# Attention and SwiGLU on one core: when each half of a batch is attended, and in which order its loads and steps are issued

## Chip, cores, metric

The kernel runs on one core of a Trainium2 chip. The metric is the device time of one execution in microseconds. The engines are TensorE (PE in the rows, PEld for its weight loads), VectorE (DVE), ScalarE (ACT), GpSimd (POOL) and SyncE (SP). GpSimd also issues almost all loads.

## The reference

Four batches, eight heads, 768 positions, head size 64. Each query sees the 8 first keys (global) and the 96 keys up to itself (local), with a slope per head times the distance as a bias; the rest is masked. The eight heads' results side by side are the 512 features of 3072 tokens, which go through a gated feed-forward layer.

```python
def _attn_ref(q, k, v, n_global, n_local) -> np.ndarray:
    ...
    scores = scale * np.matmul(q, k.transpose(0, 1, 3, 2))
    ...
    is_global = pos[None, :] < int(n_global)
    is_local = (rel >= 0) & (rel < int(n_local))
    keep = is_global | is_local
    ...
    scores = scores + bias[None, :, :, :]
    scores = np.where(keep, scores, -1000000000.0)
    scores = scores - np.max(scores, axis=-1, keepdims=True)
    a = np.exp(scores)
    a = a / (np.sum(a, axis=-1, keepdims=True) + 1e-09)
    return np.matmul(a, v).astype(np.float32)

def _moe_ref(x, w_gate, w_val, w_out) -> np.ndarray:
    g = x @ w_gate
    silu = g * (1.0 / (1.0 + np.exp(-g)))
    val = x @ w_val
    return (silu * val @ w_out).astype(np.float32)
```

## The kernel before

**Attention, in steps.** Heads go in pairs (`Pair`, four a batch). A pair's work is cut into steps, each a method: `transposes` turns q and k of two heads on TensorE, and copies bring them to `qT` and `kT` (L190, L196; L200 repeats the eight global key columns in each chunk). `scores(bk)` does a bank `bk` of three: the keys lie in seven chunks of 120 (plus the 8 global ones), each against at most 216 queries; two chunks fill bank 0, two bank 1, three bank 2. ScalarE takes the exponential (L220), and an engine `mul_eng` multiplies by a mask that holds the exponential of the bias or zero (L227, L231). `values(half, fast)` multiplies the result `at` by ones (`den`) and by V (`num`) for the queries of one half; VectorE turns `den` round, inverts it and spreads it (L259 to L262); the product goes to `xT`, on VectorE if `fast` (L267), else over a ScalarE copy to GpSimd (L270, L271). `HALF` says where a batch is cut. The first half reads banks 0 and 1, the second banks 1 and 2, so bank 1 is read by both.

**Feed-forward.** Tokens go in eight blocks of 384 (`TB`), two a batch. A block `t` is 12 times (for `f`) a gate group and a value group of four matmuls (`gate_or_val`), and from block 1 on a part of the output of block t - 1, three matmuls (`out_part`). I call each of these a group. ScalarE's tanh (L292) and VectorE (L294, L298) follow each gate and value group. Block `t` needs `xT` of its 384 tokens, all four pairs.

**What sets the order.** Engines take instructions in the order in which the program writes them. First `early` does the first half of batch 0 for the four pairs, staggered. Then the loop over `groups` writes the feed-forward groups, and puts attention steps from the list `todo` between them: each group adds its work times `quota` to `owed`, and each whole unit of `owed` takes one step. `due` holds how many steps must be through by the end of which block:

```python
due = {1: 8 + 24, 3: 24, 5: 24}
```

So the second half of batch 0 and all of batch 1 stand in blocks 0 and 1, batch 2 in blocks 2 and 3, batch 3 in 4 and 5; blocks 6 and 7 have no steps. Within a pair the steps are written one after the other (transposes, scores 0, 1, 2, values 0, 1), and a pair ends before the next begins.

**Loads.** `load_qk`, `load_v`, `load_w` and `load_wo` go through one queue of GpSimd; `loads` issues later ones at a given count 12 t + f. A `dma_start` waits until the one eight before it has landed, since eight semaphores go round (the order with its waits shows it). `load_globals` brings the eight global V rows into `vG`, and SyncE copies them into each `vS` from there.

## Time and profile before

| what | value |
|---|---|
| time, median of 3 runs | 294.28 us (293.05 to 294.45) |
| profiled execution | 293.91 us, its span 292.1 us |
| TensorE busy | 260.4 us (89%) |
| VectorE busy | 171.2 us (59%) |
| ScalarE busy | 142.8 us (49%) |
| GpSimd busy | 137.1 us (47%) |
| mean granted TensorE clock | 0.994 |
| chain that ended last | PE 64%, POOL 12%, DVE 11%, ACT 6%, DMA 4%, issue 3% |

The busy share is a mean over stages with different limits: before the first feed-forward group, in blocks with steps, in blocks without. The chain that ended last is followed back from the last instruction; it says which engine had the work that the rest waited for.

### The profile page before, as it was taken

The page shows a single profiled execution, that of the slowest core. Times are in us where ns is not written, and L with a number is a line of the kernel's source. Part 1 is how long each engine was busy: PE and PEld are TensorE (multiplying, and loading weights), DVE is VectorE, ACT ScalarE, POOL GpSimd, SP SyncE. Part 2 cuts the span into 40 slices and gives each one's busy share as a digit, 9 for nine tenths or more (in the row PEclk, how much of TensorE's full clock was granted, in tenths as well). Part 3 has the DMA queues.
Part 4 walks back from the last instruction along what each step waited for, and adds up shares of the span by engine and source line. Part 5 has one row for each costly group of instructions (what it writes and reads, how often), then busy time and mean ns, then how long its engine had stood idle before and what let it go on. Part 6 is the DMA issues. An engine that isn't in the chain of part 4 may idle for free.

```text
span 292.1 us, 5638 instructions
## 1 busy us (share of the span) xinstructions
PE 260.4 (89%) x2192; PEld 140.9 (48%) x2192; DVE 171.2 (59%) x349; ACT 142.8 (49%) x297; POOL 137.1 (47%) x162
## 2 busy tenths in 40 slices
PE   2538699799789999999989899999999999999983
PEld 1325345454445445545544545454555555555531
DVE  1627779986838565655663747474747655565510
ACT  4417644366366665556546374646475333322311
POOL 8845434057589637382988655555554100000000
PEclk9999999999899999999999999999999999999999
DMA  8999999907989110100799410101010100101111
GB/s 114 178 160 191 203 205 176 139 0 106 148 53 65 31 39 0 38 37 4 127 166 82 57 38 1 39 36 39 0 38 36 38 23 13 38 36 37 38 72 72
DMA packets 45402, 21.27 MB, mean 73 GB/s; under 512 B 28128, under 2 KB 42304, under 8 KB 45376
## 3 DMA queue, kind: packets, MB, share of 16 engines
q0 software_dynamic: 41376, 14.20, 44.9%
q1 hardware_dynamic: 4000, 6.72, 6.6%
q8 instruction: 17, 0.28, 0.4%
q14 instruction: 9, 0.07, 0.1%
HBM read 28.58 MB, written 6.29 MB: 119 GB/s over the span
## 4 chain that ended last, share of the span: by engine, by line
PE 64%; POOL 12%; DVE 11%; ACT 6%; DMA 4%; issue 3%; DVEq 0%; POOLq 0%; ACTq 0%
PE ops L307 19%; PE gps L285 17%; PE vps L285 17%; POOL vS L122 4%; PE scA L213 4%; DMA vS<-in_v_dram 4%; PE den L249 3%; ACT at L220 3%; POOL at L227 3%; PE num L249 2%; DVE rb L262 2%; POOL xT L271 2%; DVE hT L298 2%; DVE dT L259 2%; DVE sl L294 2%
## 5 line engine op out<-in xcount | busy, mean ns | idle before, releaser
L294 DVE SCALAR_TENSOR_TENSOR sl<-th,gps 128x384 f32<-128x384 f32 x96 | 52.9, 552 | 71.5 <-ACT th L292 71.1
L285 PE MATMUL gps<-xT,wg 128*128 128x384 f16 x384 | 80.6, 333 | 2.6 <-DVE hT L298 1.5
L285 PE MATMUL vps<-xT,wv 128*128 128x384 f16 x384 | 80.0, 332 | 0.6 <-DVE sl L294 0.6
L292 ACT ACTIVATE th<-gps 128x384 f32<-128x384 f32 x96 | 47.4, 494 | 63.9 <-PE gps L285 60.4
L307 PE MATMUL ops<-wo,hT 128*128 128x512 f16 x288 | 76.6, 380 | 2.1 <-ACT osb L312 2.1
L298 DVE TENSOR_TENSOR hT<-vps,sl 128x384 f16<-128x384 f32 x96 | 53.3, 555 | 11.8 <-PE vps L285 2.6
L285 PEld LDWEIGHTS <-wg 128*128 128x128 f16 x384 | 35.3, 99 | 33.3 <-issue 4.6
L285 PEld LDWEIGHTS <-wv 128*128 128x128 f16 x384 | 35.8, 99 | 28.1 <-issue 5.0
L231 POOL TENSOR_TENSOR at<-at,masks 128x432 f16<-128x432 f16 x40 | 39.3, 1003 | 19.0 <-ACT at L220 19.0
L271 POOL TENSOR_TENSOR xT<-ns,rb 128x352 f16<-128x352 f32 (+1 forms) x24 | 24.0, 1002 | 33.8 <-DVE rb L262 23.9
L307 PEld LDWEIGHTS <-hT 128*128 128x128 f16 x288 | 26.4, 98 | 27.5 <-issue 4.2
L220 ACT ACTIVATE at<-scA 128x432 f16<-128x432 f32 x48 | 25.4, 530 | 27.8 <-PE scB L213 27.8
L122 POOL DMA_DIRECT2D vS<-in_v_dram x28 | 24.8, 892 | 10.3 <-DMA wv<-in_moe_w_val_dram 2.0
L249 PE MATMUL den<-at,ones 128*64 128x216 f16 (+7 forms) x264 | 19.8, 251 | 6.5 <-POOL at L227 3.0
L220 ACT ACTIVATE at<-scB 128x432 f16<-128x432 f32 x48 | 25.5, 531 | 0.0
L227 POOL TENSOR_TENSOR at<-at,masks 128x432 f16<-128x432 f16 x24 | 24.0, 1022 | 2.1 <-ACT at L220 2.1
L312 ACT ACTIVATE osb<-ops 128x512 f32<-128x512 f32 x24 | 14.4, 599 | 20.2 <-PE ops L307 20.2
L270 ACT COPY ns<-num 128x352 f32<-128x352 f32 (+1 forms) x24 | 11.5, 479 | 24.1 <-PE num L249 20.4
L249 PE MATMUL num<-at,vS 128*64 128x216 f16 (+7 forms) x264 | 16.6, 248 | 6.1 <-DMA vS<-in_v_dram 4.7
L213 PE MATMUL scA<-qT,kT 64*128 64x216 f16 (+2 forms) x112 | 18.0, 264 | 4.3 <-POOL kT L200 2.4
L262 DVE STREAM_TRANSPOSE rb<-dR 128x352 f32<-128x352 f32 (+2 forms) x32 | 18.5, 578 | 2.7
L249 PEld LDWEIGHTS <-ones 128*64 128x64 f16 x264 | 11.7, 115 | 16.8 <-issue 12.6
(32 smaller groups left out, 179.8 us busy)
## 6 DMA issues: line engine op xcount, KB each, us to landing
out_dram<-osb SPq DMA_DIRECT2D x24, 256.0 KB, 2.0
vS<-in_v_dram POOLq DMA_DIRECT2D x24, 120.0 KB, 4.7
qst<-in_q_dram POOLq DMA_DIRECT2D x7, 384.0 KB, 5.1
kst<-in_k_dram POOLq DMA_DIRECT2D x7, 384.0 KB, 6.8
wg<-in_moe_w_gate_dram POOLq DMA_DIRECT2D x4, 384.0 KB, 11.4
wv<-in_moe_w_val_dram POOLq DMA_DIRECT2D x4, 384.0 KB, 12.6
wo<-in_moe_w_out_dram POOLq DMA_DIRECT2D x3, 512.0 KB, 16.4
qst<-in_q_dram POOLq DMA_DIRECT2D x2, 192.0 KB, 4.5
```

What stands on the lines that cost most here:

```text
L122: nc.gpsimd.dma_start(out=t[NG:NG + n, c, :, :], in_=v[b, :, KC * c:KC * c + n, :].rearrange("h p d -> p h d"))
L213: nc.tensor.matmul(sc[hi][:, col:col + n], lhsT=self.kT[r, 128 * c:128 * c + 128], rhs=self.qT[r, q0:q0 + n], start=True, stop=True)
L220: nc.scalar.activation(out=at, in_=sc[hi][:, 0:BANK], func=AF.Exp, scale=scale)
L227: mul_eng.tensor_mul(a2, a2, m[:, WIN:2 * WIN].unsqueeze(1).broadcast_to([128, 2, WIN]))
L231: mul_eng.tensor_mul(at, at, m[:, o:o + BANK])
L249: nc.tensor.matmul(dst[r, o:o + n], lhsT=ones if ones_side else vSs[b][:, c, 2 * hp + hi, :], rhs=self.at[hi, cb][:, col:col + n], start=( ...
L271: nc.gpsimd.tensor_mul(dst, ns[:, 0:n_q], rb[:, 0:n_q])
L285: nc.tensor.matmul(dst[:, 0:TB], lhsT=w[:, c, 128 * f:128 * f + 128], rhs=xT[:, c, TB * t:TB * t + TB], start=(c == 0), stop=(c == NC - 1))
L292: nc.scalar.activation(out=th, in_=dst[:, 0:TB], func=AF.Tanh, scale=0.5)
L294: nc.vector.scalar_tensor_tensor(out=sl, in0=th, scalar=1.0, in1=dst[:, 0:TB], op0=AluOp.add, op1=AluOp.mult)
L298: nc.vector.tensor_mul(hTs[t][:, f, :], dst[:, 0:TB], gv["sl"])
L307: nc.tensor.matmul(ops, lhsT=hTs[t][:, f, 128 * i:128 * i + 128], rhs=wo[:, f, :], start=(f == 0), stop=(f == NFF - 1))
```

## The change

- **Halves.** All batches are cut at 384 and not at 352 (`HALF`), so each half is exactly one feed-forward block. A half of a batch is a job of its own: `first(b)` (transposes, scores 0 and 1, values 0) and `second(b)` (scores 2, values 1). `plan` puts them into blocks: `second(0)` in block 0, `first(1)` in 1, `second(1)` and `first(2)` in 2 and 3, `second(2)` and `first(3)` in 4 and 5, `second(3)` in 6. `owed` starts at zero with each entry.
- **Pairs overlap.** Within `first(b)` a key sorts the steps: 4 hp for transposes, 4 hp + 2 and + 3 for scores, 4 hp + 5 for values. The order is T0 S0 S0 T1 V0 S1 S1 T2 V1 S2 S2 T3 V2 S3 S3 V3. Bank 1 of each pair gets a buffer of its own.
- **Engines.** Batch 0's `kT` copies go from VectorE to ScalarE; batch 1's last mask products from VectorE to GpSimd.
- **Loads.** `load_v` brings chunks 0 to 3 of one head; `load_v_rest` one chunk of all heads. At the start the loads go pair by pair, and later V loads one chunk at a time.

```diff
@@ -76,9 +76,7 @@
         chunks.append((c // 2 if c < 6 else 2,
                        [0, WIN, 0, WIN, 0, WIN, WIN + 168][c],
                        q0, min(WIN, S - q0)))
-    HALF = {0: [(0, TB), (TB, S)]}
-    for b in range(1, B):
-        HALF[b] = [(0, 352), (352, S)]
+    HALF = [(0, TB), (TB, S)]
 
     sb = ctx.enter_context(tc.tile_pool(name="sb", bufs=1))
     sb2 = ctx.enter_context(tc.tile_pool(name="sb2", bufs=2))
@@ -115,13 +113,16 @@
                 out=st[:, h0:h1, :],
                 in_=src[b, h0:h1].rearrange("h (p j) d -> p h (j d)", p=128))
 
-    def load_v(b, c0, c1):
-        t = vSs[b]
-        for c in range(c0, c1):
-            n = min(KC, S - KC * c)
-            nc.gpsimd.dma_start(
-                out=t[NG:NG + n, c, :, :],
-                in_=v[b, :, KC * c:KC * c + n, :].rearrange("h p d -> p h d"))
+    def load_v(b, h):
+        nc.gpsimd.dma_start(
+            out=vSs[b][NG:128, 0:4, h, :],
+            in_=v[b, h, 0:4 * KC, :].rearrange("(c p) d -> p c d", p=KC))
+
+    def load_v_rest(b, c):
+        n = min(KC, S - KC * c)
+        nc.gpsimd.dma_start(
+            out=vSs[b][NG:NG + n, c, :, :],
+            in_=v[b, :, KC * c:KC * c + n, :].rearrange("h p d -> p h d"))
 
 
     vG = sb.tile([NG, B, H, D], FP16, name="vG")
@@ -193,7 +194,7 @@
             k3 = self.kT.rearrange("r (c m) -> r c m", m=128)
             t3 = trk.rearrange("r (j p) -> r p j", j=J)
             for c0, c1, n in ((0, 6, KC), (6, 7, S - 6 * KC)):
-                (nc.vector.tensor_copy if b == 0 else nc.scalar.copy)(
+                nc.scalar.copy(
                     out=k3[:, c0:c1, NG:NG + n].rearrange("r c (p j) -> r c p j", j=J),
                     in_=t3[:, 20 * c0:20 * c0 + (c1 - c0) * (n // J), :].rearrange(
                         "r (c p) j -> r c p j", c=c1 - c0))
@@ -215,7 +216,7 @@
                         lhsT=self.kT[r, 128 * c:128 * c + 128],
                         rhs=self.qT[r, q0:q0 + n], start=True, stop=True)
             for hi in range(2):
-                keep = f"at{hi}{bk}b{hp}" if self.b == 0 and bk == 1 else f"at{hi}{bk}"
+                keep = f"at{hi}{bk}b{hp}" if bk == 1 else f"at{hi}{bk}"
                 at = sb2.tile([128, BANK], FP16, name="at", tag=keep, bufs=1 if "b" in keep else 2)
                 nc.scalar.activation(out=at, in_=sc[hi][:, 0:BANK], func=AF.Exp, scale=scale)
                 self.at[hi, bk] = at
@@ -232,7 +233,7 @@
 
         def values(self, half, fast):
             b, hp = self.b, self.hp
-            lo, hi_q = HALF[b][half]
+            lo, hi_q = HALF[half]
             n_q = hi_q - lo
             num = bank("num")
             den = bank("den")
@@ -314,20 +315,32 @@
             nc.sync.dma_start(out=out[r0:r0 + 128, :], in_=osb)
 
 
+    def load_pair(b, hp):
+        load_qk(b, 2 * hp, 2 * hp + 2)
+        load_v(b, 2 * hp)
+        load_v(b, 2 * hp + 1)
+
     stage(0)
     stage(1)
     load_qk(0, 0, 2)
     load_globals()
-    load_qk(0, 2, 4)
-    load_v(0, 0, 2)
-    load_qk(0, 4, 8)
-    load_v(0, 2, 4)
+    load_v(0, 0)
+    load_v(0, 1)
+    for hp in range(1, NP):
+        load_pair(0, hp)
     load_w(0)
-    load_v(0, 4, NCH)
     load_w(1)
-    load_qk(1, 0, 4)
+    for c in range(4, NCH):
+        load_v_rest(0, c)
     load_w(2)
     load_w(3)
+    load_wo(0)
+    load_qk(1, 0, 2)
+    load_wo(1)
+    load_wo(2)
+    load_qk(1, 2, 4)
+    for c in range(4):
+        load_v_rest(1, c)
 
     pairs = {(b, hp): Pair(b, hp) for b in range(B) for hp in range(NP)}
 
@@ -356,31 +369,37 @@
     state["tags"] = attn_tags
     state["n"] = 0
 
-    todo = []
-    for kind, hp in ((0, 0), (0, 1), (1, 0), (0, 2), (1, 1), (0, 3), (1, 2), (1, 3)):
-        p = pairs[0, hp]
-        todo.append((lambda p=p: p.values(1, True)) if kind else
-                    (lambda p=p: p.scores(2, nc.vector)))
-    for b in range(1, B):
+    def second(b):
+        steps = []
+        for kind, hp in ((0, 0), (0, 1), (1, 0), (0, 2), (1, 1), (0, 3), (1, 2), (1, 3)):
+            p = pairs[b, hp]
+            steps.append((lambda p=p: p.values(1, b == 0)) if kind else
+                         (lambda p=p: p.scores(2, nc.vector if b == 0 else nc.gpsimd)))
+        return steps
+
+    def first(b):
+        keyed = []
         for hp in range(NP):
             p = pairs[b, hp]
-            last = nc.vector if b == 1 else nc.gpsimd
-            todo += [p.transposes,
-                     lambda p=p: p.scores(0, nc.gpsimd),
-                     lambda p=p: p.scores(1, nc.gpsimd),
-                     lambda p=p, last=last: p.scores(2, last),
-                     lambda p=p: p.values(0, False),
-                     lambda p=p: p.values(1, False)]
-
-    loads = {0: [lambda: load_wo(0)], 1: [lambda: load_wo(1)], 2: [lambda: load_wo(2)],
-             3: [lambda: load_v(1, 0, 3)], 4: [lambda: load_v(1, 3, 5)],
-             5: [lambda: load_v(1, 5, NCH)], 7: [lambda: load_qk(1, 4, 8)]}
+            keyed += [(4 * hp, p.transposes),
+                      (4 * hp + 2, lambda p=p: p.scores(0, nc.gpsimd)),
+                      (4 * hp + 3, lambda p=p: p.scores(1, nc.gpsimd)),
+                      (4 * hp + 5, lambda p=p: p.values(0, False))]
+        return [fn for _, fn in sorted(keyed, key=lambda x: x[0])]
+
+
+    plan = [((0,), second(0)), ((1,), first(1)), ((2, 3), second(1) + first(2)),
+            ((4, 5), second(2) + first(3)), ((6,), second(3))]
+
+    loads = {13: [lambda: load_qk(1, 4, 8)]}
+    for c in range(4, NCH):
+        loads[14 + c] = [lambda c=c: load_v_rest(1, c)]
     for b in range(2, B):
-        base = 24 * (b - 2) + 12
+        base = 24 * (b - 2) + 26
         loads[base] = [lambda b=b: (stage(b), load_qk(b, 0, 4))]
         loads[base + 2] = [lambda b=b: load_qk(b, 4, 8)]
-        loads[base + 4] = [lambda b=b: load_v(b, 0, 3)]
-        loads[base + 6] = [lambda b=b: load_v(b, 3, NCH)]
+        for c in range(NCH):
+            loads[base + 3 + c] = [lambda b=b, c=c: load_v_rest(b, c)]
 
 
     NT = TOK // TB
@@ -391,14 +410,13 @@
             groups.append((t, f, 1.0, lambda t=t, f=f: gate_or_val(t, f, 1)))
             if t > 0:
                 groups.append((t, f, 1.1, lambda t=t, f=f: out_part(t - 1, f // 4, f % 4)))
-    due = {1: 8 + 24, 3: 24, 5: 24}
-    quota = {}
-    for t, n in due.items():
-        work = sum(g[2] for g in groups if g[0] in (t - 1, t))
-        for tt in (t - 1, t):
-            quota[tt] = n / (work - 3.0)
+    todo, quota = [], {}
+    for blocks, steps in plan:
+        work = sum(g[2] for g in groups if g[0] in blocks)
+        for t in blocks:
+            quota[t] = len(steps) / (work - 3.0)
+        todo.append((blocks[-1], steps))
     owed = 0.0
-    k_i = 0
     seen = set()
     for t, f, work, fn in groups:
         if (t, f) not in seen:
@@ -407,11 +425,14 @@
                 ld()
         fn()
         owed += work * quota.get(t, 0.0)
-        while owed >= 1.0 and k_i < len(todo):
-            todo[k_i]()
-            k_i += 1
+        while owed >= 1.0 and todo:
+            todo[0][1].pop(0)()
             owed -= 1.0
-    assert k_i == len(todo)
+            if not todo[0][1]:
+                assert t <= todo[0][0]
+                todo.pop(0)
+                owed = 0.0
+    assert not todo
     for i in range(3):
         for part in range(4):
             out_part(NT - 1, i, part)
```

GpSimd's queue at the start of the program, before (qst and kst are q and k of batch 0 as loaded, vS_84 its V rows):

```order
L114 DMA qst<-in_q_dram 128x2x384
L114 DMA kst<-in_k_dram 128x2x384
L130 DMA vG<-in_v_dram 8x32x64
L114 DMA qst<-in_q_dram 128x2x384
L114 DMA kst<-in_k_dram 128x2x384
L122 DMA vS_84<-in_v_dram 120x8x64 x2
L114 DMA qst<-in_q_dram 128x4x384
L114 DMA kst<-in_k_dram 128x4x384
L122 DMA vS_84<-in_v_dram 120x8x64 x2
L146 DMA wg<-in_moe_w_gate_dram 128x4x384
L146 DMA wv<-in_moe_w_val_dram 128x4x384
```

The same stretch of GpSimd's queue in the change, with line numbers of the changed file (L117 is `load_v` of one head):

```order
L112 DMA qst<-in_q_dram 128x2x384
L112 DMA kst<-in_k_dram 128x2x384
L131 DMA vG<-in_v_dram 8x32x64
L117 DMA vS_84<-in_v_dram 120x4x64 x2
L112 DMA qst<-in_q_dram 128x2x384
L112 DMA kst<-in_k_dram 128x2x384
L117 DMA vS_84<-in_v_dram 120x4x64 x2
L112 DMA qst<-in_q_dram 128x2x384
L112 DMA kst<-in_k_dram 128x2x384
L117 DMA vS_84<-in_v_dram 120x4x64 x2
L112 DMA qst<-in_q_dram 128x2x384
```

The V rows of the first two heads stand in front of the second pair's q and k; before, two whole chunks stood behind two pairs' q and k and the other two behind all of them.

ScalarE at the start, first two pairs of batch 0, before (L170 makes masks, L220 is the exponential):

```order
L170 ACTIVATE masks<-dist 128x432 x2
L190 COPY qT<-trq 128x768
L220 ACTIVATE at<-scA 128x432
L220 ACTIVATE at<-scB 128x432
L170 ACTIVATE masks<-dist 128x432 x2
L220 ACTIVATE at<-scA 128x432
L220 ACTIVATE at<-scB 128x432
L190 COPY qT<-trq 128x768
L220 ACTIVATE at<-scA 128x432
L220 ACTIVATE at<-scB 128x432
```

The same two pairs on ScalarE in the change:

```order
L171 ACTIVATE masks<-dist 128x432 x2
L191 COPY qT<-trq 128x768
L197 COPY kT_76<-trk 128x6x120
L197 COPY kT_76<-trk 128x48
L221 ACTIVATE at<-scA 128x432
L221 ACTIVATE at<-scB 128x432
L171 ACTIVATE masks<-dist 128x432 x2
L221 ACTIVATE at<-scA 128x432
L221 ACTIVATE at<-scB 128x432
L191 COPY qT<-trq 128x768
L197 COPY kT_77<-trk 128x6x120
L197 COPY kT_77<-trk 128x48
```

The two copies of kT now follow qT's on ScalarE, in front of the exponentials of that pair's scores.

GpSimd in block 1, around the second and third pair of batch 1, before (kT_77 is the second pair's; L231 and L227 are the products of scores 0 and 1, L271 the values' end):

```order
L200 COPY kT_77<-kT_77 128x7x8
L231 TENSOR_TENSOR at<-at,masks 128x432 x2
L114 DMA qst<-in_q_dram 128x4x384
L114 DMA kst<-in_k_dram 128x4x384
L227 TENSOR_TENSOR at<-at,masks 128x432 x2
L271 TENSOR_TENSOR xT<-ns,rb 128x352
L271 TENSOR_TENSOR xT<-ns,rb 128x416
L122 DMA vS_86<-in_v_dram 120x8x64 x3
L200 COPY kT_78<-kT_78 128x7x8
L231 TENSOR_TENSOR at<-at,masks 128x432 x2
L227 TENSOR_TENSOR at<-at,masks 128x432 x2
L122 DMA vS_86<-in_v_dram 120x8x64 x3
```

GpSimd in block 1 of the change, from the third pair's kT copy to the last pair's end (L201, L232, L228 and L272 are the lines L200, L231, L227 and L271 of before):

```order
L201 COPY kT_78<-kT_78 128x7x8
L272 TENSOR_TENSOR xT<-ns,rb 128x384
L123 DMA vS_85<-in_v_dram 120x8x64
L232 TENSOR_TENSOR at<-at,masks 128x432 x2
L123 DMA vS_85<-in_v_dram 120x8x64
L228 TENSOR_TENSOR at<-at,masks 128x432 x2
L201 COPY kT_79<-kT_79 128x7x8
L123 DMA vS_85<-in_v_dram 48x8x64
L272 TENSOR_TENSOR xT<-ns,rb 128x384
L232 TENSOR_TENSOR at<-at,masks 128x432 x2
L228 TENSOR_TENSOR at<-at,masks 128x432 x2
L272 TENSOR_TENSOR xT<-ns,rb 128x384
```

Each pair now ends with one L272 and not two, and another pair's kT copy stands between the products and it, but for the last pair; the loads in between are single chunks. Further up in that block, the loads of q and k of heads 4 to 7 stand between the first pair's products of scores 0 and of scores 1.

## Rows read from the trace of the kernel before

**Rows 1.** Stretches: length, PE, PEld, DVE, ACT, POOL busy us (xN), PEclk, DMA, GB/s.

```profile
33.40:40.30 6.90, 6.29 (x32) 2.50 (x29) 4.17 (x10) 2.52 (x7) 3.64 (x4) 1.00 1.31 203
40.30:63.70 23.40, 21.02 (x226) 11.68 (x222) 20.80 (x44) 11.51 (x25) 8.28 (x11) 1.00 1.14 129
63.70:105.70 42.00, 38.75 (x390) 20.60 (x387) 28.16 (x56) 24.25 (x51) 28.68 (x33) 0.96 0.61 70
77.50:81.00 3.50, 3.50 (x29) 2.16 (x28) 2.10 (x5) 1.50 (x4) 1.58 (x2) 0.51 0.84 175
105.70:231.10 125.40, 122.66 (x1066) 65.67 (x1065) 73.72 (x144) 70.13 (x147) 75.01 (x84) 1.00 0.26 45
231.10:277.80 46.70, 46.70 (x265) 25.83 (x264) 26.67 (x48) 15.37 (x30) 0.00 (x0) 1.00 0.09 35
```

**Rows 2.** Timeline, 12 to 36 us (start, length, instruction, [idle before it <- releaser]).

```profile
14.13 0.57 PE L249 MATMUL num<-at,vS 128*64 128x216 f16 x4 [1.35 <-DMA vS<-vG]
...
19.36 0.62 PE L249 MATMUL num<-at,vS 128*64 128x144 f16 x4 [4.66 <-DMA vS<-in_v_dram]
...
19.91 0.36 PE L213 MATMUL scA<-qT,kT 64*128 64x216 f16 x1
...
23.05 0.82 ACT L190 COPY qT<-trq 128x768 f16<-128x768 f16 x1
...
24.45 0.18 DVE L200 COPY kT<-kT 128x56 f16<-128x56 f16 x1
...
29.45 0.36 PE L213 MATMUL scA<-qT,kT 64*128 64x216 f16 x1 [0.21 <-DVE kT L200]
...
33.41 1.14 PE L285 MATMUL gps<-xT,wg 128*128 128x384 f16 x3
```

**Rows 3.** Timeline of TensorE, 110 to 130 us.

```profile
113.39 0.81 PE L285 MATMUL gps<-xT,wg 128*128 128x384 f16 x4
...
114.72 0.82 PE L285 MATMUL vps<-xT,wv 128*128 128x384 f16 x4
...
116.03 0.81 PE L285 MATMUL gps<-xT,wg 128*128 128x384 f16 x4
...
117.56 0.82 PE L285 MATMUL vps<-xT,wv 128*128 128x384 f16 x4
...
118.86 0.81 PE L285 MATMUL gps<-xT,wg 128*128 128x384 f16 x4
...
120.40 0.82 PE L285 MATMUL vps<-xT,wv 128*128 128x384 f16 x4
...
121.71 0.81 PE L285 MATMUL gps<-xT,wg 128*128 128x384 f16 x4
...
122.74 0.82 PE L285 MATMUL vps<-xT,wv 128*128 128x384 f16 x4
```

**Rows 4.** Timeline of TensorE, 60 to 80 us.

```profile
75.41 0.21 PE L249 MATMUL den<-at,ones 128*64 128x112 f16 x1 [0.73 <-POOL at L227]
76.52 0.21 PE L249 MATMUL den<-at,ones 128*64 128x112 f16 x1 [0.90 <-POOL at L227]
```

**Rows 5.** DMA issues, 8.4 to 9.2 us (KB each, us to landing).

```profile
vS<-in_v_dram POOLq DMA_DIRECT2D x1, 120.0 KB, 10.9
```

**Rows 6.** Instructions grouped by line and shape (busy us, mean ns of one | idle before).

```profile
L231 POOL TENSOR_TENSOR at<-at,masks 128x432 f16<-128x432 f16 x40 | 39.3, 1003 | 19.0 <-ACT at L220 19.0
...
L220 ACT ACTIVATE at<-scA 128x432 f16<-128x432 f32 x48 | 25.4, 530 | 27.8 <-PE scB L213 27.8
L122 POOL DMA_DIRECT2D vS<-in_v_dram x28 | 24.8, 892 | 10.3 <-DMA wv<-in_moe_w_val_dram 2.0 <-DVE at L231 1.9 <-DMA kst<-in_k_dram 1.8
...
L196 ACT COPY kT<-trk 128x720 f16<-128x720 f16 x12 | 9.2, 765 | 0.0
...
L196 DVE COPY kT<-trk 128x720 f16<-128x720 f16 x4 | 3.6, 902 | 5.4 <-PE trk L185 5.4
...
L196 ACT COPY kT<-trk 128x48 f16<-128x48 f16 x12 | 2.6, 218 | 0.0
```

## Prediction

> **What bounds the kernel now.** I read the page's summary first: TensorE is the busiest engine by far, so a gain must come out of its idle time, out of stretches at its lower clock, or out of the start, and not out of faster work on another engine. The busy time by stretches [rows 1] shows where to look. Up to 33.4 us attention for the first half of batch 0 runs, with TensorE mostly idle. Blocks 6 and 7 (231.1 to 277.8 us) have no gap at all: 46.70 us of 46.70 for 72 groups of matmuls, 0.65 us a group. Between them lie the blocks with attention steps in them. The timeline before 36 us [rows 2] shows the start: the values of the first head pair wait 1.35 us for the copies of vG, then 4.66 us for vS, and the scores of the second pair, next on TensorE, begin only at 19.91. From there each pair takes 4.77 us (19.91 to 29.45 for two), and the first gate matmul starts 3.96 us after the last of these, at 33.41.
>
> For the blocks I price what an inserted step adds, from pairs of neighbours in a stretch without waits [rows 3]: the start-to-start distance less the plain 0.65 us. First-half values add 1.33 - 0.65 = 0.68 us, second-half values 0.88, transposes 0.89, scores 0.38. A pair of a later batch then costs 0.89 + 3 x 0.38 + 0.68 + 0.88 = 3.59 us. With this, per stretch of [rows 1]:
> - Block 0 (33.4 to 63.7, 30.3 us): 24 groups 15.6, batch 0's second half 4 x (0.38 + 0.88) = 5.0, five steps of batch 1 2.7; loss 7.0. [...] In the rest VectorE is busy 20.80 of 23.40 us: it paces the block.
> - Block 1 (to 105.7, 42.0 us): 36 groups 23.4, steps 12.5; loss 6.1. Part is waits for GpSimd's products, 0.73 and 0.90 us one after the other [rows 4]; right behind them the granted clock falls to 0.51 for 3.5 us [rows 1], 1.7 us lost.
> - Blocks 2 to 5 (to 231.1, 125.4 us): 144 groups 93.5, steps 27.8; loss 4.1.
>
> **The start.** The changed order puts the V rows of two heads right behind their q and k, so the first pair no longer waits for the q and k of four heads and the V rows of all eight (the third V chunk, issued at 8.4 us behind those q and k, lands 10.9 us later [rows 5]). The vG copies keep their place, so the first pair's eight value matmuls can start at 14.13; the second four took 0.55 us up to the next scores (19.36 to 19.91), all eight so about 0.9: scores of the second pair at about 15.0 and not at 19.91, 4.9 us won. What is late next: its q and k now queue behind two V loads, but half of batch 0's data must land by the middle of the stretch that ended at 19.3, so a quarter more is there near 10 to 11 us, before the wait for vG ends. Against it, kT's two copies move from VectorE to ScalarE, behind qT. The copy itself is cheaper (765 ns against 902 [rows 6]), but it can only start when qT's copy ends, where VectorE copied beside it; VectorE's kT columns begin at 24.45 [rows 2], and ScalarE's chain from qT at 23.05 (0.82 + 0.77 + 0.22, with the second small copy of [rows 6]) ends at 24.86. I take 0.35 us, a little less, since copies in a row overlap by some 0.1, for each of the two periods that remain. First gate matmul: 33.4 - 4.9 + 0.7 = 29.2. Bounds: 28 if vG's copies land earlier with fewer bytes ahead of them, 31.5 if the smaller V loads land at the slower rate of the V chunks. More loads are issued on GpSimd before it can do anything else (0.89 us a V chunk [rows 6]), but in the new block 0 no step uses GpSimd: that hides them. Were the loads 20 us later they would delay block 1.
>
> **Block 0.** Five steps of batch 1 leave. TensorE loses 2.7 us of work; VectorE, which paces, loses one set of two transposes and a reciprocal and two mask products, about 2 us. So the block shrinks by 2 to 2.7 us, while the 2.7 us come back in later blocks, where TensorE paces: loss +0.4 us (bounds -2 and +1.5).
>
> **Block 1.** It now holds four pairs' transposes, two scores and first-half values: 16 steps over 34.2 groups' work, one every 2.14 groups or 1.39 us plus the step. The distances decide the waits. GpSimd multiplies four tiles a pair at 1.0 us each [rows 6], starting some 0.9 us after the first scores end (the last matmul's way out and an exponential of 0.53 [rows 6]); the fourth is done 4.95 us after. For the middle pairs scores, scores, transposes, values put the value matmuls that need it at 5.6 us: no wait. For the last pair nothing stands between second scores and values: they come at 3.4 us, 1.5 us too early. Ahead of the first pair's second products stand two q and k issues (about 0.9 us of wait), among the third pair's two V chunk issues (1.2 us). First transposes to scores 0.4, xT at the block's end 0.5. The sum is 4.5 us, and one fall of the clock as in [rows 1] at a chance of one third adds 0.5: loss 5.0 against 6.1, 1.1 won (bounds 4 and -1).
>
> **Blocks 2 to 6.** Steps are 1.93 us apart, so the same distances leave 0.4 us at each of two last pairs, 0.4 at each first transposes, 0.3 at two block ends, 0.3 for the rest: 2.5 against 4.1, 1.6 won (bounds 3 and 0). Batch 1's last masks move to GpSimd: 8 products of 1.0 us in block 2, hidden under TensorE as batch 2's and 3's are now, where 75 of 125 us of GpSimd are busy [rows 1]. Were that cover gone, they would cost up to 2 us a step. Second-half values of batch 3 go to block 6, which has no waits: pure moved work.
>
> **New work.** The first half grows from 352 to 384 queries, so a 24-column piece joins: 4 matmuls for each of 12 pairs. Second-half values have 8 more matmuls and 416 more columns than first-half ones and add 0.20 us; by that the new piece costs 0.08 us, the shorter second half gives 0.02 back: 0.7 us in all (bounds 0 and 1.2).
>
> **Sum.** -4.2 + 0.4 - 1.1 - 1.6 + 0.7 = -5.8 us. The profiled run took 293.91 us for a span of 292.1; the median is 294.28. 294.28 - 5.8 = 288.5, which I round to 288.4.
>
> [...]
>
> **Rivals.**
> - *The blocks wait less than that* (0.20). The clock doesn't fall, and in block 1 only the last pair's and the block end's waits remain (4.1 us won); blocks 2 to 6 win 2.4 and block 0 nothing: 6.5 us from the blocks and not 2.3, about 284. For it: the waits that I add up are worked out one by one, each at its nominal distance; against it: the trace has them at the same distances.
> - *GpSimd's queue takes over* (0.15). A wait moves from vS to the products: if each pair of block 1 waits as its last one does (3 x 1.5 more) and the clock falls there once (1.2 beyond the third counted), 5.7 us go: about 294, no change. For it: in the trace GpSimd's waits already lead there. Against: the middle pairs have 0.6 us to spare.
> - *The start wins little* (0.12). The engines that move data are the limit, the V waits become q and k waits: first gate matmul at 32: about 291. Against: the bytes needed by the first pair are a quarter of what it waits for now.
> - *Slower* (0.08): the clock swings. [...]
> The forecast itself has 0.45. The range 283 to 292.8 leaves out the slower rival and half of the second; within 0.5% (1.5 us, about what a measurement of this kernel can tell) I put that second rival's other part and some of the third: faster 0.81, same 0.11, slower 0.08.
>
> **What would show it.** Right: the wait for vS in front of the first pair's values gone, scores of the second pair near 15 us, first gate matmul near 29, a start of block 1 near 57, waits for GpSimd's products at the last pair of block 1. Wrong: a q or k wait at the second or third pair; block 0 longer than 29 us, or a clock below 1.00 in it; more than 7 us lost in block 1; TensorE gaps at the starts of blocks 3, 5 and 7, whose halves are now due one block ahead.

## The result, and the profile after

The changed kernel takes 284.86 us (median of 4 runs, 284.08 to 286.00) against 293.66 of the kernel before on the same chip: a ratio of 0.971, 95% interval 0.965 to 0.976. It is faster, by more than the forecast 288.4 and inside the range. The profiled execution took 286.00 us for a span of 284.21, 7.9 us less than before's 292.10.

In this table a block runs from its first gate matmul to that of the next, and the rest begins with block 7's own output; the differences are of the two profiled runs.

| us | start | block 0 | 1 | 2 | 3 | 4 | 5 | 6 | 7 | rest |
|---|---|---|---|---|---|---|---|---|---|---|
| before | 33.41 | 30.31 | 41.99 | 31.74 | 33.29 | 31.10 | 29.25 | 23.37 | 24.22 | 13.42 |
| after | 28.00 | 25.82 | 38.84 | 32.43 | 30.80 | 32.83 | 31.16 | 26.69 | 24.22 | 13.42 |
| difference | -5.41 | -4.49 | -3.15 | +0.69 | -2.49 | +1.73 | +1.91 | +3.32 | 0 | 0 |

The start gives 5.4 us, and all blocks together only 2.5: what blocks 0 and 1 save comes back in part in blocks 2 and 4 to 6, which now hold work that stood further ahead. The steps do not end with their block: those of an entry of `plan` are through before its last block ends, and the first of the next entry follow at once. In the trace one scores step of batch 1's second halves stands in block 1, two of batch 2's in block 3, and two scores steps and one values step of batch 3's in block 5. Lines of after's code stand one number higher than in the code shown (L250 for L249).

The timeline of TensorE after answers to [rows 2]:

```profile
12.82 0.72 PE L250 MATMUL num<-at,vS 128*64 128x216 f16 x8
14.26 0.36 PE L214 MATMUL scA<-qT,kT 64*128 64x216 f16 x1 [0.72 <-DVE kT L201]
...
19.15 0.36 PE L214 MATMUL scA<-qT,kT 64*128 64x216 f16 x1 [0.32 <-DVE kT L201]
...
24.04 0.36 PE L214 MATMUL scA<-qT,kT 64*128 64x216 f16 x1 [0.32 <-DVE kT L201]
...
28.00 1.14 PE L286 MATMUL gps<-xT,wg 128*128 128x384 f16 x3
...
30.02 1.48 PE L286 MATMUL vps<-xT,wv 128*128 128x384 f16 x4
```

All eight value matmuls of the first pair run in one row at 12.82, with no wait for vS and none for vG either. What is late next is kT: the scores of each following pair wait for it, 0.72 and twice 0.32 us. The first gate matmuls still last 1.14 us for three, as in the kernel with the wider order below, whose granted clock reads 0.50 there; at a granted clock of 1.00 three take 0.66 (at 30.36 us in the first kernel with spare matmuls up to the first gate matmul). So I take this stretch for half the clock, though the clock column of the windows below prints 1.00 for it.

The windows by stretch answer to [rows 1]; the columns are start:end, length, and busy time (instructions) of TensorE, its weight loads, VectorE, ScalarE and GpSimd, then granted clock, DMA share and GB/s:

```profile
28.00:34.40 6.40, 5.79 (x25) 2.42 (x23) 3.65 (x9) 2.49 (x7) 4.10 (x6) 1.00 1.36 201
34.40:53.82 19.42, 17.94 (x179) 10.68 (x178) 17.52 (x39) 7.40 (x16) 4.37 (x5) 1.00 1.27 165
53.82:92.66 38.84, 34.86 (x332) 18.14 (x330) 21.01 (x42) 22.43 (x49) 24.50 (x29) 1.00 0.31 42
...
219.88:246.57 26.69, 26.69 (x205) 14.89 (x204) 17.63 (x35) 10.71 (x22) 7.91 (x8) 1.00 0.08 31
```

From 34.4 us on the granted clock stays at 1.00: the fall of [rows 1] at 77.5 is gone. Block 6 has no idle time, so its five second-half steps are pure added work: the 3.32 us of the table. Block 1 is idle for 3.98 us. Its timeline on TensorE shows where, and answers to [rows 4]:

```profile
55.68 0.32 PE L286 MATMUL gps<-xT,wg 128*128 128x384 f16 x1 [1.20 <-DVE xT L268]
...
64.87 0.23 PE L250 MATMUL den<-at,ones 128*64 128x144 f16 x3 [0.55 <-POOL at L228]
...
81.37 0.22 PE L250 MATMUL den<-at,ones 128*64 128x144 f16 x1 [0.34 <-POOL at L228]
...
82.33 0.22 PE L250 MATMUL den<-at,ones 128*64 128x144 f16 x2 [0.73 <-POOL at L228]
...
88.25 0.22 PE L250 MATMUL den<-at,ones 128*64 128x144 f16 x1 [0.31 <-POOL at L228]
...
89.21 0.22 PE L250 MATMUL den<-at,ones 128*64 128x144 f16 x2 [0.73 <-POOL at L228]
```

Waits for GpSimd's products stand at the first pair (0.55 us), the third (1.07) and the last (1.04), none at the second. The largest single wait is for batch 0's last xT, 1.20 us behind the block's first three gate matmuls.

In blocks 2 and 4 TensorE waits for V, which the forecast did not have. Both times it is the 24-column piece that the cut at 384 added to the first half: it needs one more chunk of V, and the chunks are now loaded later, one at a time.

```profile
121.95 0.20 PE L250 MATMUL num<-at,vS 128*64 128x24 f16 x2 [0.55 <-DMA vS<-in_v_dram]
...
183.89 0.20 PE L250 MATMUL num<-at,vS 128*64 128x24 f16 x2 [0.96 <-DMA vS<-in_v_dram]
```

TensorE's timeline in stretches without waits also gives the price of the changed values steps, as [rows 3] did before: first-half values between the first two of these rows, second-half values between the last two.

```profile
140.53 0.81 PE L286 MATMUL gps<-xT,wg 128*128 128x384 f16 x4
...
141.93 0.82 PE L286 MATMUL vps<-xT,wv 128*128 128x384 f16 x4
...
230.61 0.81 PE L308 MATMUL ops<-wo,hT 128*128 128x512 f16 x3
...
232.09 0.82 PE L286 MATMUL gps<-xT,wg 128*128 128x384 f16 x4
```

Less a plain group's 0.65 us, first-half values now add 0.75 us (0.68 before) and second-half values 0.83 (0.88).

### The profile page after: what moved, and what is told of

Same layout as the page of the kernel before. It is cut to its first block, busy times and chain, and to the rows that moved or that the text cites. A ratio compares the mean times of both kernels' runs of the same rounds, so it can differ in the third digit from the quotient of the medians.

```text
span 284.2 us, 5710 instructions
## 1 busy us (share of the span) xinstructions
PE 258.3 (91%) x2240; PEld 141.4 (50%) x2240; DVE 161.3 (57%) x333; ACT 145.2 (51%) x305; POOL 149.9 (53%) x178
## 3 DMA queue, kind: packets, MB, share of 16 engines
q0 software_dynamic: 41504, 14.20, 44.3%
## 4 chain that ended last, share of the span: by engine, by line
PE 61%; POOL 13%; DMA 13%; issue 7%; ACT 3%; DVE 1%; POOLq 0%; ACTq 0%; DVEq 0%
PE ops L308 20%; PE gps L286 16%; PE vps L286 16%; DMA wo<-in_moe_w_out_dram 4%; POOL at L228 4%; DMA wv<-in_moe_w_val_dram 4%; DMA vS<-in_v_dram 3%; POOL at L232 3%; PE den L250 3%; PE scA L214 3%; PE num L250 2%; DMA qst<-in_q_dram 2%; POOL vS L123 2%; PE trq L186 1%; ACT osb L313 1%
## 5 line engine op out<-in xcount | busy, mean ns | idle before, releaser
L232 POOL TENSOR_TENSOR at<-at,masks 128x432 f16<-128x432 f16 x48 | 47.1, 1001 | 8.1 <-ACT at L221 7.6
L272 POOL TENSOR_TENSOR xT<-ns,rb 128x384 f16<-128x384 f32 x24 | 24.0, 998 | 44.7 <-DVE rb L263 28.1
L250 PE MATMUL den<-at,ones 128*64 128x216 f16 (+6 forms) x288 | 19.6, 241 | 6.5 <-POOL at L228 3.2
L271 ACT COPY ns<-num 128x384 f32<-128x384 f32 x24 | 11.5, 479 | 25.4 <-PE num L250 24.1
L228 POOL TENSOR_TENSOR at<-at,masks 128x432 f16<-128x432 f16 x24 | 23.6, 1005 | 1.5 <-ACT at L221 1.4
L123 POOL DMA_DIRECT2D vS<-in_v_dram x24 | 21.7, 905 | 3.3 <-issue 2.3
L250 PEld LDWEIGHTS <-ones 128*64 128x64 f16 x288 | 12.3, 113 | 19.9 <-issue 14.5
L260 DVE STREAM_TRANSPOSE dT<-den 128x384 f32<-128x384 f32 x32 | 18.4, 576 | 3.0 <-PE den L250 3.0
L263 DVE STREAM_TRANSPOSE rb<-dR 128x384 f32<-128x384 f32 x32 | 18.5, 578 | 2.7
```

Of the source, the lines that this page charges most:

```text
L123: nc.gpsimd.dma_start(out=vSs[b][NG:NG + n, c, :, :], in_=v[b, :, KC * c:KC * c + n, :].rearrange("h p d -> p h d"))
L228: mul_eng.tensor_mul(a2, a2, m[:, WIN:2 * WIN].unsqueeze(1).broadcast_to([128, 2, WIN]))
L232: mul_eng.tensor_mul(at, at, m[:, o:o + BANK])
L250: nc.tensor.matmul(dst[r, o:o + n], lhsT=ones if ones_side else vSs[b][:, c, 2 * hp + hi, :], rhs=self.at[hi, cb][:, col:col + n], start=( ...
L272: nc.gpsimd.tensor_mul(dst, ns[:, 0:n_q], rb[:, 0:n_q])
```

## The experiments

My theory: the start is bound by the arrival of V, and the loads' order alone wins it; the rest is a smaller gain in the blocks, limited by GpSimd's products. The rivals: the gain comes from the block plan, or the new order of steps costs what the loads win. Ratios are to the kernel before, run beside each kernel; first gate matmuls and block lengths are those of the profiled runs.

### The new loads alone, and all the rest alone

The first kernel is the one before with the V rows of each pair loaded behind its q and k. The second is the changed kernel with the old start loads:

```diff
-    load_v(0, 0)
-    load_v(0, 1)
-    for hp in range(1, NP):
-        load_pair(0, hp)
+    load_qk(0, 2, 4)
+    load_v_rest(0, 0)
+    load_v_rest(0, 1)
+    load_qk(0, 4, 8)
+    load_v_rest(0, 2)
+    load_v_rest(0, 3)
```

> The kernel before with one part of the change: batch 0 is loaded pair by pair at the start, with V rows by head (the later V loads of the other batches are cut into chunks that are issued at the same places as before). Theory A (two thirds of the gain is the start, the rest the blocks): first gate matmul near 28 us, the 20 us behind it as before, so 5 to 5.5 us below the kernel before, ratio 0.982. Theory B (the plan of halves is what wins, and an earlier start is lost again in block 0 and 1, which VectorE and GpSimd pace): first gate matmul near 28 us but block 2 starting less than 2.5 us earlier, ratio above 0.991.

> The changed kernel with the old order of loads for batch 0 (q and k of four pairs and whole V chunks, all heads at once). Theory A: the first pair's values wait for the V chunks again, first gate matmul near 33 us, 5 us above the changed kernel, ratio to the kernel before 0.99. Theory B: within 2 us of the changed kernel.

The loads alone: 287.88 us, ratio 0.979 (0.972 to 0.987). The first gate matmul comes at 27.06; blocks 0 and 1 are 0.15 us off before's each, in opposite directions, and the later ones within 0.02 us.

```profile
27.06 1.14 PE L288 MATMUL gps<-xT,wg 128*128 128x384 f16 x3
```

The rest alone: 291.50, ratio 0.989 (0.981 to 0.998), first gate matmul at 33.93, blocks as in the changed kernel to about 0.2 us, but for block 0, which is 0.6 us shorter. TensorE's timeline of this second kernel has the old waits back:

```profile
14.37 0.57 PE L250 MATMUL num<-at,vS 128*64 128x216 f16 x4 [1.59 <-DMA vS<-vG]
...
19.49 0.33 PE L250 MATMUL num<-at,vS 128*64 128x144 f16 x2 [4.55 <-DMA vS<-in_v_dram]
```

The two parts add up within their intervals: 0.979 x 0.989 = 0.969, and the changed kernel, run again, gave 0.968. About two thirds of the gain is the loads. The vG copies also land late again with the old order (the 1.59), so this wait hung on the loads as well.

> The changed kernel itself, beside the next three on one chip: ratio to the kernel before between 0.965 and 0.976.

The changed kernel again: 284.74 us, ratio 0.968 (0.965 to 0.971), first gate matmul at 27.02.

### kT's copies back on VectorE

```diff
-                nc.scalar.copy(
+                (nc.vector.tensor_copy if b == 0 else nc.scalar.copy)(
```

> The changed kernel with batch 0's kT copies back on VectorE. The prediction's term (the copies on ScalarE, behind qT's, cost 0.35 us in each of two periods): first gate matmul 0.7 us earlier than in the changed kernel, 27.3 us. Rival (VectorE's copies wait behind its mask products, and delay the turning of the denominators): period longer than 4.89 us, first gate matmul at 28 us or later.

284.69 us against 284.74: no price that shows. The second, third and fourth pair's scores stand 5.08 and 4.58 us apart here, and 4.89 twice in the changed kernel, 0.06 us a period more; my 0.35 us a period is not there.

### The pairs one after the other

```diff
-                      (4 * hp + 2, lambda p=p: p.scores(0, nc.gpsimd)),
-                      (4 * hp + 3, lambda p=p: p.scores(1, nc.gpsimd)),
-                      (4 * hp + 5, lambda p=p: p.values(0, False))]
+                      (4 * hp + 1, lambda p=p: p.scores(0, nc.gpsimd)),
+                      (4 * hp + 2, lambda p=p: p.scores(1, nc.gpsimd)),
+                      (4 * hp + 3, lambda p=p: p.values(0, False))]
```

> The changed kernel with the pairs of a first half one behind the other (transposes, scores 0, scores 1, values), nothing between scores 1 and values. Theory A (the distance between scores and values decides the waits in the blocks): all four pairs of block 1 wait for GpSimd's products as the last one does in the changed kernel, some 1 us more for each of three pairs in block 1 and 0.3 to 0.5 us in blocks 3 and 5, and the scores wait for kT: 4 to 7 us above the changed kernel, more if the clock falls. Rival (the overlap does nothing, GpSimd's total work sets the pace): within 1 us of the changed kernel.

300.3 us, ratio 1.020 (1.013 to 1.027): slower than the kernel before, and more than twice the 4 to 7 us that I gave without a fall of the clock. TensorE's waits for the products, in us in total, times and longest, first in the changed kernel:

```profile
PE den L250 <- POOL at L228: 3.2, 7, 0.7
```

The same in this kernel, and below it the windows of block 1 and of the two new stretches at the low clock:

```profile
PE den L250 <- POOL at L228: 11.0, 17, 1.8
```

```profile
53.41:98.79 45.38, 37.22 (x332) 18.99 (x331) 21.21 (x42) 22.68 (x49) 24.67 (x29) 0.96 0.26 36
65.00:68.40 3.40, 3.40 (x24) 1.62 (x25) 1.66 (x4) 0.48 (x1) 1.00 (x1) 0.51 0.86 132
...
191.20:198.10 6.90, 5.01 (x31) 2.52 (x33) 1.43 (x3) 0.97 (x3) 1.91 (x2) 0.51 0.57 37
```

The product waits grow from 3.2 to 11.0 us, and the granted clock falls to 0.51 in stretches of 3.4 and 6.9 us. In the second of these TensorE also waits 2.20 us for V. The kernel before, also pair after pair, had the last third of scores between second scores and values; the halves take that step away, and without the overlap nothing stands there. The halves need the overlap: this is the slower side of the change.

### The old due times

Batch 1's both halves are due by the end of block 1 again, the others likewise, with the loads moved ahead to match:

```diff
-    plan = [((0,), second(0)), ((1,), first(1)), ((2, 3), second(1) + first(2)),
-            ((4, 5), second(2) + first(3)), ((6,), second(3))]
+    plan = [((0, 1), second(0) + first(1) + second(1)), ((2, 3), first(2) + second(2)),
+            ((4, 5), first(3) + second(3))]
```

> The changed kernel with the old due times: both halves of batch 1 in blocks 0 and 1, of batch 2 in 2 and 3, of batch 3 in 4 and 5, none in block 6, loads moved up accordingly; start, cut at 384 and overlap of pairs as in the change. Theory A (VectorE and GpSimd pace blocks 0 and 1, so work that leaves them is won there and costs only its TensorE time later): 1.5 to 4 us above the changed kernel, with blocks 0 and 1 losing 3 us more than the moved TensorE time. Rival (only the order of steps within the blocks counts, not the block that they are in): within 1 us.

290.65 us, ratio 0.985 (0.978 to 0.993), 5.9 us over the changed kernel, more than the 1.5 to 4 expected. Blocks 0 and 1 are 30.84 and 42.85 long, about as before. Its waits on TensorE:

```profile
PE den L250 <- POOL at L228: 4.9, 8, 0.7
...
PE den L250 <- POOL at L232: 2.0, 4, 0.7
```

So the due times are what the block gain of 2.5 us hangs on: with pairs overlapped but everything due early, the products are waited for 6.9 us, and blocks 0 to 6 take 223.6 us together, 2.6 more than before.

### A wider order: three kernels

The forecast's weak places are the first and the last pair of block 1. Here more steps stand between a pair's scores and values (T transposes, A and B scores, V values), and the load of batch 1's q and k of heads 4 to 7 comes earlier, ahead of the products in GpSimd's queue:

```diff
-            keyed += [(4 * hp, p.transposes),
...
+        order = "T0 T1 A0 B0 T2 A1 B1 V0 T3 A2 B2 V1 A3 B3 V2 V3"
...
-    loads = {13: [lambda: load_qk(1, 4, 8)]}
+    loads = {9: [lambda: load_qk(1, 4, 8)]}
```

> The changed kernel with the first halves written T0 T1 A0 B0 T2 A1 B1 V0 T3 A2 B2 V1 A3 B3 V2 V3 (A and B are scores 0 and 1), so that at least two steps stand between a pair's second scores and its values, one for the last pair, and with the load of q and k of heads 4 to 7 of batch 1 moved up into block 0. Theory A (distance decides): the waits for GpSimd's products fall from 3.2 us to under 1 us, 1.5 to 3 us below the changed kernel. Rival (GpSimd's work per block sets when the last values are ready, so the wait only moves to the last pair or to the block's end): within 0.7 us of the changed kernel.

278.47 us, ratio 0.947 (0.944 to 0.950), 6.3 us under the changed kernel, twice the highest that I expected. Block 1 shrinks from 38.84 to 35.40, and blocks 2 to 5 together by 2.3 us (126.6 in the changed kernel's second profile, 124.3 here, with no idle time of TensorE left in them). The window of block 1, and what is left of the waits in it:

```profile
52.35:87.75 35.40, 33.98 (x332) 17.86 (x330) 21.11 (x42) 22.58 (x49) 22.98 (x27) 1.00 0.26 38
```

```profile
PE gps L286 <- DVE xT L268: 1.2, 1, 1.2
PE den L250 <- POOL at L228: 0.2, 1, 0.2
```

Then the order alone, with the load at its old place:

> The kernel with the wider order of steps (278.47 us) made two edits to the changed kernel: the order of the steps of a batch's first half, and the load of batch 1's q and k of heads 4 to 7 four group pairs earlier, so that GpSimd issues it before it has a product to make. Here the order alone is kept and the load is back at its place. Theory A, the order is what counts (two or three TensorE steps between a pair's second scores and its values): 278 to 279.5 us, no wait for a product above 0.3 us in block 1, block 1 at 35 to 36.5 us. Theory B, the load's place is what counts (GpSimd's two issues ahead of the first pair's products, about 1.5 us, push every later product back): 281 to 284 us, product waits of 0.5 us and more at the first two pairs of block 1.

283.28 us, ratio 0.963 (0.960 to 0.966). This kernel and the later ones, but for the first with spare matmuls, ran on two other chips (the kernel before took 294.15 and 294.30 us there, and 294.05 beside the wider order). The time is theory B's, but not its reason: the product waits are 0.2 us as well. In block 1 TensorE's third transposes now come earlier than their data:

```profile
64.39 0.53 PE L186 MATMUL trq<-ident,qst 128*64 128x128 f16 x12 [1.53 <-DMA qst<-in_q_dram]
66.32 0.53 PE L186 MATMUL trk<-ident,kst 128*64 128x128 f16 x12 [1.41 <-DMA kst<-in_k_dram]
```

```profile
66.90:70.30 3.40, 3.40 (x14) 1.24 (x13) 1.11 (x2) 1.71 (x4) 0.23 (x1) 0.50 0.00 0
```

The two waits cost 2.9 us, and the half clock behind them 1.7 by estimate (half of the 3.40 us at 0.50): 4.6 of the 4.8 us between the two kernels. Blocks 2 to 5 are as short as with both edits. So the order takes the product waits away, and the earlier load takes away the wait that the order brings. The load alone wasn't run.

### What limits block 0

The forecast said that VectorE paces block 0. The first test leaves out part of the computation: the eight mask products of batch 0's last third of scores, work of VectorE in this block.

```diff
             for hi in range(2):
+                if self.b == 0 and bk == 2:
+                    break
```

> The kernel with the wider order, without the mask products of batch 0's last third of scores: this leaves out part of the computation, eight products on VectorE in block 0, some 3.0 us of its work at 0.38 us each. Theory A, VectorE paces block 0 (17.69 of 19.00 us busy in it from 33 us on, TensorE 17.53): block 0 falls from 25.06 us to 23.0 to 23.7, since TensorE's own idle time in it is 2.08 us, and the run by 1.4 to 2 us to about 276.7. [...]

278.02 us (277.58 to 278.87) against 278.47. For comparison, block 0 of the kernel with the wider order in a window, and its part at the low clock:

```profile
27.29:52.35 25.06, 22.98 (x203) 12.84 (x201) 21.04 (x47) 9.63 (x22) 10.24 (x13) 0.90 1.47 196
27.29:32.20 4.91, 4.30 (x19) 1.73 (x18) 2.64 (x6) 0.98 (x4) 3.64 (x5) 0.50 1.50 195
```

Block 0 of this kernel, and its part behind the low clock:

```profile
27.39:52.92 25.53, 23.65 (x203) 13.08 (x201) 18.97 (x39) 9.87 (x23) 10.24 (x13) 0.88 1.45 196
...
33.70:52.92 19.22, 17.95 (x180) 10.63 (x178) 15.78 (x32) 7.39 (x16) 6.38 (x8) 1.00 1.47 195
```

VectorE is busy 2.07 us less than in the kernel with the wider order (21.04), and block 0 is 25.53 us long instead of 25.06. The low clock lasted to 33.7 and not to 32.2, which at a granted clock of 0.50 is worth 0.75 us; without it the block would have gained some 0.3 us, by this estimate. VectorE follows.

The second test keeps the clock up with spare matmuls in the start, which add no result; they take one of the start's eight result banks. A first try, on the changed kernel, put three behind transposes and values only:

> The changed kernel with three spare matmuls of 216 columns behind each transposes and values step of the start (their result is not used), where TensorE waits. [...] Rival (VectorE paces block 0, so a faster TensorE there only waits): block 1 starts less than 1.2 us earlier.

285.14 us: no gain, but the clock was not held. TensorE's timeline, and the window behind it:

```profile
26.52 1.18 PE L250 MATMUL den<-at,ones 128*64 128x216 f16 x8 [1.76 <-DVE at L232]
```

```profile
26.80:33.60 6.80, 6.17 (x34) 2.95 (x34) 3.70 (x9) 2.87 (x10) 4.07 (x6) 0.50 1.47 199
```

The clock fell right behind the 1.76 us wait for the last pair's products. So the next kernel, on the one with the wider order, fills that wait too:

```diff
+    spare = ps.tile([128, 512], FP32, name="spare", tag="o0")
+
+    def keep_busy(n):
+        for _ in range(n):
+            nc.tensor.matmul(spare[0:64, 0:WIN], lhsT=ones, rhs=masks[:, 0, 0:WIN],
+                             start=True, stop=True)
...
                 early(hp, s)
+                keep_busy([3 if hp > 0 else 0, 0, 16 if hp + 1 == NP else 0,
+                           14 if hp + 1 == NP else 6][s])
```

> The kernel with the wider order, and spare matmuls of 216 columns into an unused bank wherever TensorE waits in the start: three behind each transposes but the first, six behind the values of pairs 0 to 2, sixteen between the last pair's second scores and its values, fourteen behind those values. They add no result. [...] Theory B, VectorE paces block 0 (21.04 us of work in 25.06 us): block 0 24 to 25 us, the run 277.5 to 278.5. [...]

277.68 us (276.56 to 278.77): unclear as a time, clear by parts. The clock fell once more in the start, behind a wait of 1.46 us for k, but it was up again from 21.6 us on. Block 0 falls to 22.55 us, where theory B had 24 to 25, but the first gate matmul comes at 30.36. TensorE's timeline and windows:

```profile
17.60 0.53 PE L186 MATMUL trk<-ident,kst 128*64 128x128 f16 x12 [1.46 <-DMA kst<-in_k_dram]
...
19.35 1.27 PE L363 MATMUL spare<-masks,ones 128*64 128x216 f16 x6
```

```profile
18.20:21.60 3.40, 3.40 (x37) 2.67 (x34) 2.08 (x6) 1.56 (x5) 3.40 (x5) 0.50 1.27 162
30.36:52.91 22.55, 21.02 (x201) 12.32 (x201) 20.07 (x44) 9.22 (x20) 9.05 (x12) 1.00 1.44 196
```

The last kernel has three spare matmuls, and not six, behind the values of pairs 0 to 2.

> As the kernel with spare matmuls up to the first gate matmul, but with three and not six of them behind the values of pairs 0 to 2. In that run block 0 was 2.51 us shorter (22.55 against 25.06) while the first gate matmul came 3.07 us later (30.36 against 27.29): the third pair's transposes waited 1.46 us for k, the clock then fell from 18.2 to 21.6 us, and six spare matmuls took 1.27 us there ahead of the scores. Theory A, the late start came from that wait and from the spare matmuls ahead of the scores, and both are not part of the clock's price: first gate matmul at 27.3 to 28.5, block 0 again about 22.5 us, the run 275.5 to 277. Theory B, any spare work in the start comes back as a later first gate matmul: 29.5 us or later, and 277.5 to 278.5.

276.41 us (276.22 to 278.19), ratio 0.941 (0.936 to 0.946): theory A, and the lowest time of this study. Window of block 0, and the first gate and value matmuls on the timeline:

```profile
27.82:50.39 22.57, 21.03 (x202) 12.33 (x202) 20.09 (x45) 9.23 (x20) 10.25 (x13) 1.00 1.44 197
```

```profile
27.82 1.04 PE L286 MATMUL gps<-xT,wg 128*128 128x384 f16 x4
28.70 0.81 PE L286 MATMUL vps<-xT,wv 128*128 128x384 f16 x4
```

The first value matmuls take 0.81 us for four where after they took 1.48, and block 0 is 2.5 us shorter with nearly the same work of VectorE in it (20.09 us busy, against 21.04). The wider order's block 0 lay 4.91 us at a granted clock of 0.50, and half of that, its price by estimate, is 2.5 us: the clock's level, not VectorE, was the price. All of it shows in the block, but only 2.1 us in the median, since the first gate matmul came 0.5 us later here.

## Why the prediction was right, point by point

The sign and the main cause were right: the V wait in the start is the largest term, and the experiment with the loads alone shows it. The size was short: the profiled runs differ by 7.9 us, the sum said 5.8 (294.28 less 5.8 is 288.5; the 288.4 is a slip). The blocks together came out 2.5 us shorter where 1.6 were forecast, in part by luck: too little was forecast for blocks 0 and 1, too much for blocks 2 to 6.

- **Start, -4.2 forecast, -5.4 measured.** The step that was off is "the vG copies keep their place, so the first pair's eight value matmuls can start at 14.13". They started at 12.82 with no wait for these copies, whose wait came back with the old loads (1.59 us); the lower bound of 28 us, given for that case, is what came. From there the kT chain paces, as said, but its move to ScalarE cost nothing that shows, and not 0.7 us. In the other kernels with these loads, without six spare matmuls, the first gate matmul lies between 27.02 and 28.16.
- **Block 0, loss 7.4 forecast, 5.2 measured** (25.82 less 15.6 and 5.0). Against that, 1.2 us of wait stand just behind the border: the last xT is waited for in block 1. The step that failed is "in the rest VectorE is busy 20.80 of 23.40 us: it paces the block" (the rest is 40.30 to 63.70 in [rows 1]). VectorE's busy share was high because the block was full for both engines; in the kernel with the wider order, taking its work away gave some 0.3 us, taking the low clock away 2.5. In the first 6.9 us of this block before, three gate matmuls last 1.14 us [rows 2], and later four last 0.81 [rows 3]. Half of that stretch, 3.4 us by estimate, went to the low clock, and the sum has nothing of it as something to win.
- **Block 1, loss 5.0 forecast, 5.5 measured** (38.84 less 23.4, four pairs at 0.89 + 2 x 0.38 + 0.75 = 2.40, and 0.38 for the scores step of a second half). The waits stand where they were put, and are smaller: first pair 0.55 (0.9), second none, third 1.07 (1.2), last 1.04 (1.5). The xT at the block's border is larger, 1.20 against 0.5. The clock did not fall. For both blocks together the loss went from 13.1 to 10.7 us: 2.4 won, 0.7 forecast. TensorE's idle time in the two blocks hardly changed, 6.2 us before [rows 1] and 6.1 after: 1.7 of the 2.4 us is the fall of the clock that did not come, and the waits mostly moved. The loads alone, with the old plan, had such a fall in block 1 (four gate matmuls took 1.46 us at 72.76, and 0.82 at 66.38), the rest alone had none (at most 0.82 us in its block 1). It does not come in every execution of the kernel before: one of 292.74 us has a mean clock of 1.000.
- **Blocks 2 to 6, loss 2.5 forecast, 3.7 measured** (153.91 less 116.9 for the groups and 33.3 for the steps, at the prices of the changed kernel): 0.4 won against 1.6. What the forecast had at nothing are the waits for V in blocks 2 and 4, 0.55 and 0.96 us.
- **New work, +0.7 forecast, about +0.2 measured:** 0.07 us more for the first half of each of 12 pairs, 0.05 less for the second. The step that was off is that the shorter second half gives only 0.02 back. The terms of the blocks, -2.4 - 0.4 + 0.2, make -2.6 against -2.48 measured, with the prices rounded.

Of the rivals, the one that GpSimd's queue takes over did not come, but its place was right: the kernel with the pairs one after the other shows that it decides as soon as nothing stands between scores and values (11.0 us of waits), and the wider order with its earlier load shows that its remains were worth 3.4 us in block 1. The slower rival, the swinging clock, did not come either. What the rows show is this, a fall being a granted clock of 0.50 or 0.51: in both profiled runs of the changed kernel no fall after the first groups of block 0 (behind them four gate or value matmuls took at most 0.82 us), though TensorE waited 1.20 us once, and 0.34 and 0.73 in a row; in the kernel before one behind 0.73 and 0.90 in a row [rows 4]; one behind 1.53 and 1.41 where the load came too late; one behind 1.46 us in the start with the spare matmuls, and one behind 1.76. The length of one wait alone doesn't order these (0.90 with a fall, 1.20 without), and what does was not tried. Block 0 of the changed kernel kept a granted clock of 1.00 from 34.4 us on, with three idles in it of 0.67, 0.48 and 0.33 us (17.94 of 19.42 us busy).

## What to carry to other kernels

Load each piece of the data in the order in which its first consumer needs it, also across tensors: here that gave two thirds of the gain, by itself. When work is split, look at what stood between producer and consumer by chance: the split took a step out of the gap, and only the new order put another into it. An engine that is busy nine tenths of a block need not pace it, as VectorE in block 0 of the wider order (17.69 of 19.00 us from 33 us on); take some of its work away before you believe it, and look at the clock of the engine beside it.

## What the runs showed of the hardware that I had not expected

VectorE's small copy of kT's first columns takes 0.18 us [rows 2]. In the changed kernel two of them take far longer. VectorE's and GpSimd's timelines:

```profile
8.48 0.43 DVE L201 COPY kT<-kT 128x56 f16<-128x56 f16 x1 [6.27 <-ACT kT L197]
...
13.63 0.58 DVE L201 COPY kT<-kT 128x56 f16<-128x56 f16 x1 [0.97 <-ACT kT L197]
```

```profile
8.15 0.77 POOL L112 DMA_DIRECT2D qst<-in_q_dram  x1
...
12.55 1.65 POOL L117 DMA_DIRECT2D vS<-in_v_dram  x2
```

They end at 8.91 and 14.21, where a GpSimd DMA issue ends (8.92 and 14.20). The scores of the next pair wait for this copy (the row at 14.26), so it cost the second pair 0.40 us here. But a copy is not always longer there. With kT's copies back on VectorE it stands at the same place of the same two issues and takes 0.18 us; VectorE's and GpSimd's rows of that kernel:

```profile
13.62 0.18 DVE L201 COPY kT<-kT 128x56 f16<-128x56 f16 x1
```

```profile
12.56 1.64 POOL L117 DMA_DIRECT2D vS<-in_v_dram  x2
```

All 14 traces of this study together: 14 such copies began in the first 0.18 us of a GpSimd DMA issue, and each took 0.18 us. Five began 0.27 to 0.29 us into one, and two of them took longer. All 18 that began 0.31 us or more into one, with more than 0.2 us of it left, ended within 0.03 us of its end. So more loads issued from GpSimd can cost a pair of the start some tenths of a microsecond (0.40 here), and whether they did hung, in these traces, on where in an issue the copy fell. Why a copy ends with an issue is not shown. No run here moved the issues to another queue to test it.
